# w3 times w_last by halves of the sum, with the second half's stores adding in DRAM

## The chip, the cores and the metric

The kernel runs on one core of one Trainium2 chip. The metric is the device time of one execution in microseconds (us). Beside the times there is one profiled execution, and every duration below comes from it.

## The reference

Three stages follow one another. Attention over 4 batches and 12 heads (448 positions, 64 features a head) with RMS-normalised queries and keys; a two-layer network with a leaky ReLU (768 to 2048 to 768); and a second one, whose end matters here:

```
a = x @ w1
b = x @ w2
h = a * b @ w3
return (h @ w_out).astype(np.float32)
```

All is float32, for 1792 tokens. `w3` is 1024 x 1024, and this last `w_out`, called `w_last` in the kernel, is 1024 x 768. Nothing stands between the two, so the kernel forms the product w3 times w_last once, from the weights alone, and later multiplies `a * b` by it. The change is in how that product is formed.

## The kernel before

Weights come as float64 words. Each tile of them is converted on the chip: ScalarE scales both halves of the word in place (L456, L460), VectorE shifts one and adds the other (L458, L462), and the float32 result `raw` is split into a rounded high part and the rest, a low part. For w3 these are `wh` (ScalarE, L491) and `wl` (VectorE, L198). For w_last they are `lasth` (GpSimd, L109) and `lastl` (VectorE, L198), which stay in SBUF until the product is done. Every product is then three matmuls: high by high, high by low, low by high (`group`, L532 to L549).

The product w3 times w_last has 8 row blocks of 128 rows (k). Its sum runs over 8 tiles of w_last (j). A row block's share of w3 comes as two pieces, `w3t[k, 0]` for the tiles j = 0 to 3 and `w3t[k, 1]` for j = 4 to 7, each 128 x 512. The 768 columns are cut in two (e), 384 each, one PSUM bank (`pw`) each. So one piece of w3 gives 24 matmuls of 384 columns, and the whole product 384 of them.

`combine_weights` (L552 to L579) goes row block by row block: both banks of a block stay open over both halves of the sum. Before the first piece it takes w_last's tiles 0 to 3, before the second piece tiles 4 to 7. A finished bank is copied to SBUF by ScalarE (`wo`, L575; two buffers) and stored to the DRAM tensor `wc` by a DMA that GpSimd issues (L576). `wc` is read again only in the later stages (L703, L972).

This work runs beside attention. Attention goes by pairs of heads: transposed keys (`pk`, L219), scores (`ps`, L127), the minimum and scaling on VectorE (L264), the exponential on ScalarE (L273), transposes of the result (`pt`, L307) and the product with the values (`po`, L127). ScalarE rounds the keys (`kh`, L228) and VectorE forms their rest (`kl`, L229). `fill` (L1020) deals the matmuls of the product out over attention's steps 1 to 11 by a count of their cost, and a scheduler with its own model of time then sets the final order on each engine. Each engine works through its queue in that order. The order of the weight loads and conversions is that of the list given to `Weights` (L1050 to L1063): a tile is converted when its turn in the list comes, and its load is issued some tiles ahead.

Of the kernel before, what the change touches and what calls it, by code (L numbers as in the profile page):

```python
# [11 lines left out]
AF = mybir.ActivationFunctionType  # L12
ALU = mybir.AluOpType
# [6 lines left out]
DM, FF, F2 = 768, 2048, 1024  # L20
# [6 lines left out]
K2 = F2 // P  # L27
WT = DM
PB = 2
KH2 = K2 // 2  # L30
# [18 lines left out]
def attention_then_moe(  # L49
# [22 lines left out]
    nc = tc.nc  # L72
# [19 lines left out]
    def bank(name):  # L92
        return psum.tile([P, 512], F32, tag="ps", name=name)
# [438 lines left out]
    def group(ws, ps, n, w, xs, first=True, last=True, on=False):  # L532

        wh, wl = w

        def matmul(a, x, begin, end):
            nc.tensor.matmul(ps[:, :n], a, x, start=begin, stop=end, skip_group_check=on)  # L540

        for k, (xh, xl) in enumerate(xs):
            end = last and k == len(xs) - 1
            h, l = (w[k] if isinstance(w, list) else w[:, k] for w in (wh, wl))
            matmul(h, xh, first and k == 0, False)
            matmul(h, xl, False, False)
            matmul(l, xh, False, end)
            ws.pump()
            yield 3 * n * NS  # L549


    def combine_weights(ws, pool, hi, lo):  # L552
        def last(half):
            for _ in range(KH2):
                while ws.ready <= ws.taken:
                    with tc.high_priority(CONVERT_PRIORITY if ws.ready else 0):
                        next(ws.pieces)
                    yield CONVERT_NS
                ws.take()

        n = DM // 2
        for k in range(K2):
            ps = [bank("pw") for _ in range(2)]
            for half in range(2):
                if k == 0:
                    yield from last(half)
                w = ws.take()
                js = range(half * KH2, (half + 1) * KH2)
                for e in range(2):
                    cols = slice(e * n, (e + 1) * n)  # L570
                    xs = [(hi[:, j, cols], lo[:, j, cols]) for j in js]
                    yield from group(ws, ps[e], n, w, xs, first=half == 0, last=half == 1)
            for e in range(2):
                o = pool.tile([P, n], F32, tag="o", name="wo", bufs=2)
                nc.scalar.activation(o, ps[e][:, :n], AF.Copy)  # L575
                nc.gpsimd.dma_start(  # L576
                    wc[3 * e : 3 * e + 3, :, k].rearrange("m p c -> p m c"),
                    o.rearrange("p (m c) -> p m c", m=3),
                )  # L579


# [96 lines left out]
    def sources(plan):  # L678

        for f, bs, g in plan:  # L680
            if f is first_mlp:
                tiles = [w_in[g * KG + m] for m in range(KG)] + [w_out[g, m] for m in range(NO)]
            else:
                tiles = [w12[g * KH2 + m // 2, m % 2] for m in range(2 * KH2)]
            if (f, g) in kept:
                yield from ((k, False, None, None) for k in again[f, g])
            else:
                twice = sum(x[0] is f and x[2] == g for x in plan) > 1
                names = ("", "_h", "_l") if twice else ("",)
                ks = [  # L690
                    [
                        dram.tile([P, w.shape[1] // 2], F32, name=f"kept_{f.__name__}{g}_{i}{e}")
                        for e in names
                    ]
                    for i, w in enumerate(tiles)
                ]
                kept[f, g] = [k[0] for k in ks]
                again[f, g] = [tuple(k[1:]) for k in ks]
                yield from ((w, True, k, None) for w, k in zip(tiles, ks))
            if f is second_mlp:  # L700
                for m in range(NO):
                    w = wc[m, :, g * KH2 : (g + 1) * KH2].rearrange("p k c -> p (k c)")
                    yield w, False, None, None  # L703
# [10 lines left out]
    last = {}  # L714
# [247 lines left out]
    def last_sources():  # L962
        def pairs(x):
            return list(zip(x[::2], x[1::2]))

        for g in range(NG):
            yield from pairs(kept[first_mlp, g][:KG])
            yield from ([x] for x in kept[first_mlp, g][KG:])
        for g in range(2):
            yield from pairs(kept[second_mlp, g])  # L970
            js = slice(g * KH2, (g + 1) * KH2)
            yield from ([wc[m, :, js].rearrange("p k c -> p (k c)")] for m in range(NO))  # L972
# [47 lines left out]
    def fill(gen, total, span, until, begin=0):  # L1020

        spent, n = 0.0, 0
        done = False
        while True:
            at = next(steps, None)
            n += 1
            while not done and spent < total * (n - begin) / span:
                c = next(gen, None)
                if c is None:
                    done = True  # L1030
                else:
                    spent += c
            if at is None or at == until:
                break
        for _ in gen:
            pass

    parts_of = [(first_mlp, g) for g in range(NG)] + [(second_mlp, g) for g in range(2)]
    early = [(f, (0,), g) for f, g in parts_of[:EARLY]]
    late = [(f, (1,), g) for f, g in parts_of[:EARLY]]  # L1040
# [6 lines left out]
    with tc.tile_pool(name="comb", bufs=1) as pool:  # L1047
        hi = pool.tile([P, K2, DM], F32R, name="lasth")
        lo = pool.tile([P, K2, DM], F32R, name="lastl")
        ws = Weights(  # L1050
            [
                w
                for k in range(K2)
                for h in range(2)
                for w in [
                    (w_last[j], True, None, (hi[:, j], lo[:, j]))
                    for j in range(h * KH2, (h + 1) * KH2)
                    if k == 0
                ]
                + [(w3t[k, h], True, None, None)]  # L1060
            ]
            + list(sources(early + late))
        )  # L1063
        blocks = Blocks(list(last_sources()))
        n = slots[1] - slots[0]
        fill(combine_weights(ws, pool, hi, lo), comb_ns, n * per_slot, slots[1], slots[0] * per_slot)
# [4 lines left out]
    n = PB * H + 2  # L1071
# [50 lines left out]
```

## Time and profile before

| what | value |
|---|---|
| median of 3 runs | 1182.44 us (1179.35 to 1185.0) |
| the profiled execution, its own time | 1181.46 us |
| its span, first to last instruction | 1179.7 us |
| TensorE (PE) busy | 1140.0 us, 97% |
| VectorE (DVE) busy | 705.0 us, 60% |
| ScalarE (ACT) busy | 657.8 us, 56% |
| GpSimd (POOL) busy | 228.8 us, 19% |

TensorE is busy nearly all the time, so the time is close to the sum of its work. What it loses is found in the few stretches where it stands or runs at the lower of its clocks. PEld is its loading of weights, which runs beside the matmuls. A matmul's shown duration contains its way through the array, so the spacing between starts, not the duration, says how fast a row of matmuls goes.

### The profile page before, as it was taken

The page shows a single profiled execution, that of the slowest core. Times are in us where ns is not written, and L with a number is a line of the kernel's source. Part 1 is how long each engine was busy: PE and PEld are TensorE (multiplying, and loading weights), DVE is VectorE, ACT ScalarE, POOL GpSimd, SP SyncE. Part 2 cuts the span into 40 slices and gives each one's busy share as a digit, 9 for nine tenths or more (in the row PEclk, how much of TensorE's full clock was granted, in tenths as well). Part 3 has the DMA queues.
Part 4 walks back from the last instruction along what each step waited for, and adds up shares of the span by engine and source line. Part 5 has one row for each costly group of instructions (what it writes and reads, how often), then busy time and mean ns, then how long its engine had stood idle before and what let it go on. Part 6 is the DMA issues. An engine that isn't in the chain of part 4 may idle for free.

```text
span 1179.7 us, 16734 instructions
## 1 busy us (share of the span) xinstructions
PE 1140.0 (97%) x6096; PEld 959.2 (81%) x6096; DVE 705.0 (60%) x1336; ACT 657.8 (56%) x1347; POOL 228.8 (19%) x337
## 2 busy tenths in 40 slices
PE   3899999999999999999999999999999999899998
PEld 2588866666788888888888888879999999799997
DVE  7976576877523667567545543493455556854553
ACT  7968687987644565666556543355443344443331
POOL 3331344554212232345222011000000000000000
PEclk9899999999999999999999999999999999899999
DMA  9655375885965446346342421441221212102112
GB/s 298 215 167 197 120 269 198 289 303 180 312 193 172 154 140 214 120 141 206 119 124 86 170 83 46 133 161 34 75 65 43 81 42 67 53 31 90 50 36 103
DMA packets 74979, 164.51 MB, mean 139 GB/s; under 512 B 13968, under 2 KB 42384, under 8 KB 74896
## 3 DMA queue, kind: packets, MB, share of 16 engines
q1 hardware_dynamic: 55392, 80.06, 22.2%
q10 hardware_dynamic: 10800, 48.76, 12.2%
q0 software_dynamic: 8704, 34.61, 7.8%
q8 instruction: 48, 0.79, 0.3%
q14 instruction: 35, 0.29, 0.1%
HBM read 120.46 MB, written 42.95 MB: 139 GB/s over the span
## 4 chain that ended last, share of the span: by engine, by line
PE 86%; DVE 7%; DMA 5%; issue 1%; ACT 1%; SPq 0%; POOL 0%; DVEq 0%
PE ps_mm L540 33%; PE ps_o L540 13%; PE ps_b L540 10%; PE ps L127 6%; PE pt L307 6%; PE po L127 6%; PE pw L540 5%; PE ps_c L540 5%; PE ps_a L540 2%; DVE ol L198 1%; DMA wh<-kept_first_mlp_h 1%; DMA w<-w_last 1%; DVE raw L462 1%; DMA w<-w_in 1%; PE pk L219 1%
## 5 line engine op out<-in xcount | busy, mean ns | idle before, releaser
L198 DVE TENSOR_TENSOR wl<-raw,wh 128x512 fp32r<-128x512 f32 (+1 forms) x136 | 108.3, 798 | 124.3 <-ACT wh L491 81.0
L264 DVE TENSOR_SCALAR_CACHE_REDUCE p<-ps,rs 112x448 f32<-112x448 f32 x192 | 122.3, 679 | 42.1 <-PE ps L127 41.9
L540 PE MATMUL ps_mm<-xl,wh 128*128 128x448 f32 x384 | 146.2, 381 | 0.0
L273 ACT ACTIVATE p<-p,low 112x448 f32<-112x448 f32 x192 | 126.9, 665 | 30.0 <-DVE p L264 30.0
L540 PE MATMUL ps_mm<-xh,wh 128*128 128x448 f32 x384 | 141.2, 368 | 1.9 <-DMA wh<-kept_first_mlp_h 1.9
L540 PE MATMUL ps_mm<-xh,wl 128*128 128x448 f32 x384 | 141.6, 369 | 0.7 <-DMA wl<-kept_first_mlp_l 0.7
L540 PE MATMUL ps_mm<-gl,wh 128*128 128x448 f32 x288 | 109.6, 381 | 0.0
L540 PE MATMUL ps_mm<-gh,wh 128*128 128x448 f32 x288 | 106.1, 370 | 0.5 <-DMA wh<-kept_first_mlp_h 0.5
L540 PE MATMUL ps_mm<-gh,wl 128*128 128x448 f32 x288 | 105.7, 367 | 1.0 <-DMA wl<-kept_first_mlp_l 1.0
L540 PE MATMUL ps_o<-gl,wh 128*128 128x448 f32 x288 | 104.1, 366 | 0.0
L307 PEld LDWEIGHTS pt<-ident,p 112*112 112x112 f32 x768 | 82.3, 137 | 26.5 <-issue 8.5
L456 ACT ACTIVATE w<-w 128x768 f32<-128x768 f32 (+1 forms) x80 | 63.8, 798 | 70.5 <-DMA w<-w_out 31.7
L307 PE MATMUL pt<-ident,p 112*112 112x112 f32 x768 | 96.6, 267 | 5.2 <-DVE kl L229 2.8
L540 PE MATMUL ps_o<-gh,wl 128*128 128x448 f32 x288 | 100.6, 366 | 0.0
L540 PE MATMUL ps_o<-gh,wh 128*128 128x448 f32 x288 | 99.2, 365 | 0.0
L491 ACT ACTIVATE wh<-raw 128x512 fp32r<-128x512 f32 (+1 forms) x84 | 59.4, 708 | 55.8 <-PE ps_mm L540 51.4
L540 PEld LDWEIGHTS ps_mm<-xl,wh 128*128 128x128 f32 x384 | 72.4, 188 | 12.3 <-issue 7.2
L540 PEld LDWEIGHTS ps_mm<-xh,wh 128*128 128x128 f32 x384 | 72.3, 188 | 9.0 <-DVE qk_sb L173 2.2
L746 ACT ACTIVATE wh<-raw 128x512 fp32r<-128x512 f32 (+1 forms) x52 | 36.3, 698 | 76.9 <-PE ps_b L540 33.5
L540 PEld LDWEIGHTS ps_mm<-xh,wl 128*128 128x128 f32 x384 | 72.5, 189 | 7.6 <-issue 1.6
L127 PE MATMUL po<-pth,v_sb 112*64 112x448 f32 x384 | 77.5, 546 | 1.0 <-ACT pth L105 1.0
L462 DVE CUSTOM_DVE_ANT_0 raw<-w,raw 128x1536 uint16<-128x1536 uint16 (+1 forms) x80 | 74.4, 933 | 2.0 <-ACT w L460 0.5
(139 smaller groups left out, 2524.3 us busy)
## 6 DMA issues: line engine op xcount, KB each, us to landing
w<-w_in ACTq DMA_DIRECT2D x16, 768.0 KB, 5.3
w<-w_out ACTq DMA_DIRECT2D x24, 512.0 KB, 3.9
w<-w ACTq DMA_DIRECT2D x16, 768.0 KB, 4.6
qk_sb<-qk SPq DMA_DIRECT2D x48, 224.0 KB, 4.3
w<-w3t ACTq DMA_DIRECT2D x15, 512.0 KB, 5.1
kept_first_mlp<-raw POOLq DMA_DIRECT2D x16, 384.0 KB, 5.6
kept_first_mlp<-raw POOLq DMA_DIRECT2D x24, 256.0 KB, 3.1
kept_second_mlp<-raw POOLq DMA_DIRECT2D x16, 384.0 KB, 2.9
```

The costliest lines, as they stand in the source:

```text
L127: one = nc.tensor.matmul(out, a, x, start=begin, stop=end)
L198: e.tensor_tensor(out, x, y.bitcast(F32), op=ALU.subtract)
L219: nc.tensor.transpose(pk[:, c * CP : (c + 1) * CP], kn[:, c].rearrange("p h d -> p (h d)"), ident[:CP, :CP],)
L264: nc.vector.tensor_scalar(p, ps[c % 2][e], x["scale"][:, e, c : c + 1], None, op0=ALU.mult, op1=ALU.min, accum_out=low,)
L273: exps[t] = nc.scalar.activation(p, p, AF.Exp, bias=low, scale=-1.0, accum_out=x["sums"][:, e, c : c + 1])
L307: nc.tensor.transpose(pt[:, c * CP : (c + 1) * CP], h["p"][c][:, kc * CP : (kc + 1) * CP], ident[:CP, :CP],)
L456: nc.scalar.activation(h, h, AF.Prelu, scale=2.0**-112, alpha=2.0**32)
L462: nc.vector.tensor_tensor(top, top, low, op=ALU.add)
L491: self.rounded = nc.scalar.activation(flat[0], x, AF.Copy)
L540: nc.tensor.matmul(ps[:, :n], a, x, start=begin, stop=end, skip_group_check=on)
L746: nc.scalar.activation(parts[0], x, AF.Copy)
```

## The change

The product goes in two passes. The first pass takes all 8 row blocks with w_last's tiles 0 to 3, the second all 8 with tiles 4 to 7. Only tiles 0 to 3 stand before the first piece of w3; tiles 4 to 7 are dealt out one by one before later pieces of the first pass (`late.pop(0)` at k = 2, 4, 6 and 7). A bank now holds one half of the sum for 12 matmuls and is copied out after them. So there are 32 copies and 32 stores, where there were 16 of each. The first pass stores plainly, the second with `accum_op=add`, which adds to what is in DRAM. The matmuls are the same 384.

```
     def combine_weights(ws, pool, hi, lo):
-            ps = [bank("pw") for _ in range(2)]
-            for half in range(2):
-                if k == 0:
-                    yield from last(half)
-                w = ws.take()
...
+    def combine_order():
+        early = list(range(KH2))
+        late = list(range(KH2, K2))
+        yield early, 0, 0
+        for k in range(1, K2):
+            yield ([late.pop(0)] if k % 2 == 0 or k == K2 - 1 else []), k, 0
+        for k in range(K2):
+            yield [], k, 1
...
+            w = ws.take()
+            js = range(half * KH2, (half + 1) * KH2)
             for e in range(2):
+                ps = bank("pw")
+                cols = slice(e * n, (e + 1) * n)
+                xs = [(hi[:, j, cols], lo[:, j, cols]) for j in js]
+                yield from group(ws, ps, n, w, xs)
                 o = pool.tile([P, n], F32, tag="o", name="wo", bufs=2)
-                nc.scalar.activation(o, ps[e][:, :n], AF.Copy)
+                nc.scalar.activation(o, ps[:, :n], AF.Copy)
+                sums = dict(accum_op=ALU.add) if half else {}
                 nc.gpsimd.dma_start(
                     wc[3 * e : 3 * e + 3, :, k].rearrange("m p c -> p m c"),
                     o.rearrange("p (m c) -> p m c", m=3),
+                    **sums,
                 )
...
-                for k in range(K2)
-                for h in range(2)
...
+                for js, k, half in combine_order()
+                for w in [(w_last[j], True, None, (hi[:, j], lo[:, j])) for j in js]
+                + [(w3t[k, half], True, None, None)]
```

On VectorE, right behind the low part of the first piece of w3. In these names `raw` from `w64` is a tile of w_last, `raw` from `w3` a piece of w3. Before:

```order
L198 TENSOR_TENSOR wl_479<-raw_469,wh_478 128x512
L458 TENSOR_SCALAR raw_527<-w64_400 128x768
L198 TENSOR_TENSOR lastl_156<-raw_490,lasth_155 128x768
L107 COPY pth_534<-pt_535 112x448
L173 TENSOR_TENSOR qk_sb_292<-qk_sb_292,rs_375 112x2x4x64
L462 ISA raw_527<-w64_400,raw_527 128x1536
L458 TENSOR_SCALAR raw_563<-w64_463 128x768
```

The same place now:

```order
L198 TENSOR_TENSOR wl_477<-raw_469,wh_476 128x512
L458 TENSOR_SCALAR raw_544<-w64_384 128x768
L458 TENSOR_SCALAR raw_581<-w3_386 128x512
L107 COPY pth_534<-pt_535 112x448
L462 ISA raw_544<-w64_384,raw_544 128x1536
L462 ISA raw_581<-w3_386,raw_581 128x1024
L198 TENSOR_TENSOR wl_526<-raw_489,wh_525 128x512
```

Before, tiles of w_last follow, and the second piece's `wl` stands 28 rows further on. Now it stands 6 rows further on.

On TensorE, at the product with the values of the first pair of heads (`po`) and what follows it. Before:

```order
L127 MATMUL po<-pth,v_sb 64x448 x8
L307 MATMUL pt<-ident,p 112x112 x16
L127 MATMUL ps<-kh,qh 112x448
L540 MATMUL pw<-lasth,wh 128x384
L540 MATMUL pw<-lastl,wh 128x384
```

Now:

```order
L127 MATMUL po<-pth,v_sb 64x448 x8
L307 MATMUL pt<-ident,p 112x112 x3
L540 MATMUL pw<-lasth,wh 128x384
L540 MATMUL pw<-lastl,wh 128x384
L540 MATMUL pw<-lasth,wl 128x384
```

Before, 24 matmuls of the product stand ahead of this `po`, and 24 ahead of the scores (`ps`) of the third pair. Now 60 stand ahead of the one, 84 ahead of the other, and some stand between the transposes.

On ScalarE, the copies `wo` and what they wait for (DMASW is the landing of an earlier store). Before, the second block's two copies:

```order
L575 ACTIVATE wo_928<-pw_775 128x384 [waits DMASW0_49,PE_49,Activation_49]
L152 ACTIVATE sq_974<-qk_sb_820 112x512 [waits DMAHW1_49,Activation_49]
L491 ACTIVATE wh_958<-raw_944 128x512 [waits PE_49]
L437 DMA w3_1021<-w3t 128x1024 [waits DMAHW7_49]
L575 ACTIVATE wo_931<-pw_776 128x384 [waits DMASW1_49,PE_49]
```

Now, where the third pair's exponentials run:

```order
L579 ACTIVATE wo_760<-pw_723 128x384 [waits DMASW3_49]
L273 ACTIVATE p_802,sum_785<-p_802,low_803 112x448 [waits DVE_49]
L273 ACTIVATE p_806,sum_785<-p_806,low_807 112x448 [waits DVE_49]
L579 ACTIVATE wo_823<-pw_763 128x384 [waits DMASW4_49,Activation_49]
L273 ACTIVATE p_810,sum_785<-p_810,low_811 112x448 [waits DVE_49]
L491 ACTIVATE wh_1005<-raw_987 128x512 [waits PE_49]
L437 DMA w3_1050<-w3t 128x1024 [waits DMAHW5_49]
L273 ACTIVATE p_814,sum_785<-p_814,low_815 112x448 [waits DVE_49]
L579 ACTIVATE wo_846<-pw_826 128x384 [waits DMASW5_49,PE_49,Activation_49]
```

There are twice as many copies, and each waits for the landing of the store two before it, with attention's exponentials queued behind.

## Rows read from the trace of the kernel before

**Rows 1.** Page: busy us, share of span, instructions of each engine.

```profile
PE 1140.0 (97%) x6096; PEld 959.2 (81%) x6096; DVE 705.0 (60%) x1336; ACT 657.8 (56%) x1347; POOL 228.8 (19%) x337
```

**Rows 2.** Stretches: us, length, busy us of each engine, PE clock, DMA share, GB/s.

```profile
38.30:49.10 10.80, 10.76 (x64) 6.75 (x60) 10.80 (x19) 10.80 (x26) 4.55 (x4) 1.00 0.38 133
49.10:51.80 2.70, 0.00 (x0) 0.00 (x0) 2.70 (x5) 1.73 (x4) 1.20 (x1) 1.00 0.89 188
51.80:58.60 6.80, 6.57 (x23) 4.53 (x24) 6.80 (x16) 5.03 (x10) 1.91 (x2) 0.50 0.47 148
...
62.00:160.40 98.40, 98.40 (x596) 80.18 (x594) 60.66 (x130) 70.42 (x158) 27.89 (x44) 1.00 0.56 180
```

**Rows 3.** Waits of PE, 0 to 62 us: in total, times, longest.

```profile
PE pt L307 <- DVE kl L229: 2.8, 1, 2.8
...
PE ps L127 <- ACT wh L491: 0.2, 1, 0.2
```

**Rows 4.** Chain that ended last, 52 to 54 us: start, us, what.

```profile
52.40 0.64 ACT wh L491
53.04 0.70 PE ps L127
```

**Rows 5.** Timeline of PE: start, us, engine, line, operation, count.

```profile
41.80 0.44 PE L540 MATMUL pw<-lasth,wh 128*128 128x384 f32 x1
42.17 0.45 PE L127 MATMUL ps<-kh,qh 64*112 64x448 f32 x1
...
54.15 0.52 PE L540 MATMUL pw<-lastl,wh 128*128 128x384 f32 x1
54.47 0.52 PE L540 MATMUL pw<-lasth,wh 128*128 128x384 f32 x1
...
155.14 0.33 PE L540 MATMUL pw<-lasth,wl 128*128 128x384 f32 x1
155.31 0.34 PE L540 MATMUL pw<-lasth,wh 128*128 128x384 f32 x1
155.58 0.45 PE L127 MATMUL ps<-kh,qh 64*112 64x448 f32 x1
```

**Rows 6.** Timeline of DVE: first and second piece's low part, a wide tile's add.

```profile
36.80 0.69 DVE L198 TENSOR_TENSOR wl<-raw,wh 128x512 fp32r<-128x512 f32 x1
...
39.91 0.95 DVE L462 CUSTOM_DVE_ANT_0 raw<-w,raw 128x1536 uint16<-128x1536 uint16 x1
...
55.55 0.68 DVE L198 TENSOR_TENSOR wl<-raw,wh 128x512 fp32r<-128x512 f32 x1
```

**Rows 7.** Timeline of ACT, 47 to 56 us.

```profile
47.18 0.68 ACT L228 ACTIVATE kh<-pk,gqk 128x448 fp32r<-128x448 f32 x1
...
48.34 0.73 ACT L273 ACTIVATE p<-p,low 112x448 f32<-112x448 f32 x1
...
48.99 0.65 ACT L152 ACTIVATE sq<-qk_sb 112x512 f32<-112x512 f32 x1
49.52 0.69 ACT L152 ACTIVATE qk_sb<-qk_sb 112x512 f32<-112x512 f32 x1
...
54.96 0.68 ACT L456 ACTIVATE w<-w 128x512 f32<-128x512 f32 x1
55.53 0.67 ACT L460 ACTIVATE w<-w 128x512 uint32<-128x512 uint32 x1
```

**Rows 8.** Copies and stores of the product: ns min/median/max, first and last start.

```profile
L575 ACT ACTIVATE wo<-pw x16: 461/470/493, 60.9 to 163.1; 128x384 f32<-128x384 f32 x16
L576 POOL DMA_DIRECT2D wc<-wo x16: 748/796/993, 61.7 to 164.4; - x16
...
DMA to landing us min/median/max: 2.5/4.4/8.1
```

**Rows 9.** DMA issues, 0 to 165 us: KB each, median us to landing.

```profile
w<-w_last ACTq DMA_DIRECT2D x4, 768.0 KB, 8.7
```

More of the change, by code (lines that the diff above doesn't have):

```diff
@@ L549, in group @@
             yield 3 * n * NS
+    def combine_order():
[6 more added lines that the diff above has]
+            yield [], k, 1
     def combine_weights(ws, pool, hi, lo):
-        def last(half):
-            for _ in range(KH2):
+        n = DM // 2
+        for new, k, half in combine_order():
+            for _ in new:
                 while ws.ready <= ws.taken:
@@ L559, in last @@
                 ws.take()
-        n = DM // 2
-        for k in range(K2):
-            ps = [bank("pw") for _ in range(2)]
-            for half in range(2):
-                if k == 0:
-                    yield from last(half)
-                w = ws.take()
[L568 to L572, printed above, removed]
+            w = ws.take()
+            js = range(half * KH2, (half + 1) * KH2)
             for e in range(2):
+                ps = bank("pw")
+                cols = slice(e * n, (e + 1) * n)
+                xs = [(hi[:, j, cols], lo[:, j, cols]) for j in js]
+                yield from group(ws, ps, n, w, xs)
                 o = pool.tile([P, n], F32, tag="o", name="wo", bufs=2)
-                nc.scalar.activation(o, ps[e][:, :n], AF.Copy)
+                nc.scalar.activation(o, ps[:, :n], AF.Copy)
+                sums = dict(accum_op=ALU.add) if half else {}
                 nc.gpsimd.dma_start(
@@ L1052, in attention_then_moe @@
                 w
-                for k in range(K2)
-                for h in range(2)
[L1055 to L1060, printed above, removed]
+                for js, k, half in combine_order()
+                for w in [(w_last[j], True, None, (hi[:, j], lo[:, j])) for j in js]
+                + [(w3t[k, half], True, None, None)]
             ]
```

## Prediction

> **What bounds the kernel now.** The page comes first. TensorE (PE) is busy 97% of the span [rows 1], so a change gains only where PE stands or runs slowly, and the next view is the one by stretches [rows 2]. From 62 to 160.4 us, where most of this product is done, PE is busy in all of 98.40 us at a granted clock of 1.00: nothing to gain there. Before it there are two places. Between 49.1 and 51.8 us PE does nothing, and from 51.8 to 58.6 its granted clock is 0.50, the lower of its two levels (1.2 GHz). The matmuls show it: two of 384 columns start 0.32 us apart at 54.15, and 0.17 us apart at 155.14 [rows 5]. The waits name what PE stood for: a transpose 2.8 us for `kl`, the third pair's keys on VectorE, and the scores behind it 0.2 us more, with `wh`, the second piece of w3, ending last [rows 3]. The chain of what ended last runs into PE at 53.04 from `wh` [rows 4]. VectorE is busy throughout (10.80 of 10.80, 2.70 of 2.70): four tiles of w_last pass through it there. From the first piece's low part at 36.80 to the second's at 55.55 are 18.75 us [rows 6], and with the first piece's 24 matmuls done PE has nothing of the product to fill a gap with.
>
> **The change part by part.** All sums are made against the profiled execution, 1181.46 us, of which its span is 1179.7; that is 0.98 us under the median of 1182.44.
>
> What goes: the standing, 2.8 + 0.2 = 3.0 us [rows 3], and the slow stretch after it, in which 6.57 us of work [rows 2] would take half: 3.3 us. Together 6.3 us, if PE has work through the whole of it.
>
> Has it? By the order now, 84 matmuls of the product stand ahead of the third pair's scores instead of 24. These 60 take 60 x 0.17 = 10.2 us at the upper clock [rows 5], more than the 6.3 that are to be filled. Their weights: the second piece's low part stands 6 rows behind the first's on VectorE. At no more than 0.95 us each, the widest add there [rows 6], it ends by 36.80 + 0.69 + 6 x 0.95 = 43.2 us, where PE still has the first piece and attention. So late `wh` is no longer what PE meets.
>
> What is late next is ScalarE. Before, it finishes the third pair's `kh` from 47.18 us [rows 7]. By the order now, it does more ahead of that: 3 narrow tiles at 2 x 0.57, 4 roundings (0.57 each, as one pass over such a tile), 3 copies at 0.47 [rows 8], 2 exponentials at 0.65 and 2 squares at 0.53, the spacings of rows 7: 3.4 + 2.3 + 1.4 + 1.3 + 1.1 = 9.5 us, so `kh` starts near 56.7 and `kl` is ready near 58. PE reaches these scores at 53.0 [rows 4] less the 3.0 of standing plus 10.2: 60.2 us. Two us are in hand. That is little, because ScalarE must wait for loads there; I charge 1.0 us for short waits of PE, between 0 (all within the two us) and 6.3 (the gap comes back whole).
>
> What is added. Sixteen copies of 0.47 us on ScalarE, 7.5 us: it stands 28 of the 98.4 us in which most of them fall [rows 2], so nothing; without that cover 7.5. Sixteen stores that GpSimd takes 0.80 us each to issue [rows 8], 12.8 us beside some 70 in which it stands [rows 2]: nothing. Behind them on GpSimd are queued the small factors of the next pairs and the low parts `ql` and `xl`, which are needed a pair later. More changes of PE between the product and attention: 98 instead of 90 up to its last matmul. One costs 0.27 - 0.17 = 0.10 us [rows 5], so 0.8 us. SP's queue issues the same loads; of ScalarE's, pieces of w3 go out earlier and tiles of w_last later, out of a full stretch into one at a DMA share of 0.38 [rows 2]: nothing.
>
> The open cost is the added wait. There are two buffers `wo`, and each copy waits for the landing of the store two before it, with attention's exponentials queued behind on ScalarE. Two copies can't follow faster than copy, issue and landing: 0.47 + 0.80 + 4.4 = 5.7 us [rows 8]. What PE leaves for it follows from the copies before: sixteen, each of a bank of 24 matmuls, start from 60.9 to 163.1 us [rows 8], so 24 matmuls, now two banks, come every 102.2 / 15 = 6.8 us, with attention between. The plain stores of the first pass fit. The second pass's stores add in DRAM, and no row shows such a store. It can't gain. The nearest row is the plain store of the same 192 KB on the same queue, 4.4 us; at the upper end I set twice that, 8.8, because it also reads what it writes. At 4.4 it costs nothing; at 8.8 two copies take 10.1 us, 3.3 more than PE leaves, over eight such pairs 26.4 us. I take 5.5, near the plain store's row: 6.8 us, just fitting.
>
> Sum: -6.3 + 0.8 + 1.0 = -4.5 us, or 1177.0 us for a profiled execution and 1178.0 us against the median.
>
> **The rivals.** *PE had more slack than its busy time shows.* In the 10.80 us from 38.3 PE counts as busy for 10.76, but its weight loads fill 6.75 us, 63%; from 62 to 160.4 they fill 80.18 of 98.40, 81% [rows 2]. At 81% the same loads fit in 8.3 us, so 2.5 us of that stretch are short waits between matmuls. Rows 5 have one: from `pw` at 41.80 to `ps` at 42.17 are 0.37 us, where the same step takes 0.27 at 155.31. With work of the product at hand they would go too: -4.5 - 2.5 = -7.0, 1175.4 us. Against it: the kinds of matmul differ between the stretches (short transposes load more often), and attention's own chain through ScalarE and VectorE stays.
>
> The Trainium skill has this as a rule ("Perfetto Trace Analysis", section "Identifying the Most-Contended Engine"): matmul busy time is a poor measure of how near TensorE is to its peak, and the busy share of its weight loads a better one. The two stretches of rows 2 agree with it as far as 10.76 of 10.80 busy goes with 63% of loading; by busy time alone the sum stays at -4.5, by the rule it is -7.0.
>
> *ScalarE takes the place of VectorE.* From 38 us to the third pair's scores it has no free time by the count above, and it must wait there for tiles of w_last whose loads are now issued later, one at a time; such a load takes 8.7 us to land [rows 9]. Two such waits of 3 us use up the 2 us in hand and the gain: about 0, 1182 us, give or take 2. For it speaks how full the engine is; against it, that the DMA engines are less busy by then (0.38).
>
> *The adding stores bind.* Place: the copies of the second pass on ScalarE, with attention's exponentials behind them. The price is 8 x (L + 1.27 - 6.8) for a landing of L us. It begins at L = 5.5, has used up the gain of 4.5 at 6.1, and is slower by over 0.5% from 6.8. At 8.8 it is -4.5 + 26.4 = +22: 1204 us. For it: the slowest plain store took 8.1 us [rows 8], and an adding one does more. Against it: the banks PE can fill meanwhile, and that two stores are under way at once.
>
> **How the numbers follow.** The forecast has 0.40, the first rival 0.27, the second 0.15, the third 0.18. A measurement of this kernel can tell about 0.5%, 5.9 us, from no change. Faster by more than that is most of the first rival (0.25) and the better edge of the forecast (0.05): 0.30. Slower is most of the third rival (0.14) and a little of the second (0.01): 0.15. The rest, 0.55, is within. The likeliest case alone spans 1175.5 to 1180 us. The range goes from 1173 (below it 0.05, the edge of the first rival) to 1192 (above it 0.10, where adding stores land after 7.3 us or more).
>
> **What would show it.** Right: no standing of PE at 49 us; its granted clock at 1.00 from 40 us on; 84 matmuls of the product ahead of the third pair's scores, which start near 60 us; the last matmul of the product near 156 us (before, the stretch of rows 2 that ends at 160.4 ends with it); 32 copies, the later stores landing within 6 us; the orders behind it shifted as a whole. Wrong: a wait of PE for ScalarE's `kh` or exponentials, or for a bank, between 45 and 75 us (second rival); ScalarE's copies waiting for DMA after 90 us and PE idle behind them (third); weight loads above 75% before 62 us and a gain of 7 (first).

## The result, and the profile after

The changed kernel takes 1190.35 us (median of 11 runs, 1187.18 to 1194.3), the kernel before 1182.44 us over as many runs on that chip (1178.07 to 1187.82). The ratio is 1.0064, with a 95% interval of 1.0048 to 1.0080: 7.6 us slower, where 4.5 us less were forecast. The time lies within the range that was given, but on the other side of the kernel before. The profiled execution took 1190.86 us, its span 1189.1 us.

First the page's busy times and its row of GpSimd's own DMA queue (packets, MB, share of the 16 engines' span), which answer to [rows 1]:

```profile
PE 1141.7 (96%) x6096; PEld 958.9 (81%) x6096; DVE 700.7 (59%) x1336; ACT 663.4 (56%) x1363; POOL 251.8 (21%) x353
...
q0 software_dynamic: 15104, 37.76, 10.3%
```

TensorE (PE) has the same work. GpSimd's queue moves 3.1 MB more, as 16 more stores should, but in 15104 packets instead of 8704. Next the stretches, those of [rows 2] and two more (columns as there):

```profile
20.00:40.00 20.00, 9.57 (x40) 6.47 (x39) 15.68 (x33) 15.61 (x31) 5.18 (x5) 0.50 0.90 275
...
38.30:49.10 10.80, 10.80 (x58) 9.53 (x57) 8.70 (x16) 10.80 (x25) 4.20 (x7) 0.81 0.83 242
49.10:51.80 2.70, 2.70 (x17) 2.70 (x17) 2.70 (x7) 2.70 (x6) 1.83 (x3) 1.00 0.90 352
51.80:58.60 6.80, 6.80 (x41) 4.42 (x40) 4.88 (x10) 6.80 (x16) 2.77 (x3) 1.00 0.57 190
...
112.00:168.00 56.00, 51.98 (x302) 41.20 (x301) 34.95 (x71) 37.89 (x88) 31.07 (x38) 0.95 0.90 191
```

and the two added stretches in the kernel before:

```profile
20.00:40.00 20.00, 13.54 (x64) 10.30 (x63) 20.00 (x38) 20.00 (x43) 7.91 (x10) 1.00 1.04 349
112.00:168.00 56.00, 56.00 (x342) 44.00 (x341) 36.13 (x78) 38.64 (x88) 21.48 (x33) 1.00 0.57 191
```

Three things can be read. What the forecast wanted is there: PE no longer stands from 49.1 to 51.8 us, and from 51.8 to 58.6 its granted clock is 1.00 (2.4 GHz). But ahead of that, from 20 to 40 us, ScalarE (ACT) is busy for 15.61 us instead of 20.00 and VectorE for 15.68: 4 us are lost before the product begins. And from 112 to 168 us PE loses 4.0 us that it did not lose before, at a DMA share of 0.90 instead of 0.57, and its granted clock is 0.95 in the mean instead of 1.00. Of the times that the prediction named, the third pair's scores start at 63.59 us (forecast near 60).

**The start.** ScalarE's timeline (start, us; ACTq rows are DMA issues; in brackets the idle time and what ended it), then two links of the chain that ended last:

```profile
14.94 0.38 ACTq L437 DMA_DIRECT2D w<-w3t  x1
15.54 0.33 ACTq L437 DMA_DIRECT2D w<-w_last  x1
17.37 0.34 ACTq L437 DMA_DIRECT2D w<-w3t  x1
20.02 4.12 ACTq L437 DMA_DIRECT2D w<-w3t  x2
24.19 0.67 ACT L273 ACTIVATE p<-p,low 112x448 f32<-112x448 f32 x1 [3.41 <-DMA v_sb<-v]
...
36.57 0.63 ACT L491 ACTIVATE wh<-raw 128x512 fp32r<-128x512 f32 x1
```

```profile
9.20 14.59 DMA v_sb<-v
23.81 0.33 ACTq L437
24.19 0.18 ACT p L273
```

The second of the two issues at 20.02 does not go out until `v`, issued by SP at 9.20 us, has landed at 23.79. While this load instruction waits, all of ScalarE stands: the exponential behind it starts 3.41 us late. (`v` itself landed hardly earlier before, at 23.52 us; what came earlier in ScalarE's queue is the load that waits for it.) The same stretch before holds only this ahead of 23 us, and `wh` comes 4.06 us sooner:

```profile
15.49 0.38 ACTq L437 DMA_DIRECT2D w<-w_last  x1
21.09 0.38 ACTq L437 DMA_DIRECT2D w<-w3t  x1
21.59 0.40 ACTq L437 DMA_DIRECT2D w<-w3t  x1
...
32.51 0.65 ACT L491 ACTIVATE wh<-raw 128x512 fp32r<-128x512 f32 x1
```

So by 20.5 us ScalarE has sent for 2.25 MB (three pieces of w3 and a tile of w_last) instead of 0.75, into engines that are already full (a DMA share of 1.05 from 14 to 21 us, before 1.03), and the second pair's `qk` share these engines with them (its last one lands at 30.94 us, before at 26.78). The Trainium skill ("DMA: Bandwidth & Descriptors", section "Issuing engines are not separate DMA queues") says that starting transfers from several engines saves only the time of the issue; the trace agrees in that SP's `qk`, issued at 13.00 us and so ahead of ScalarE's pieces, took 17.94 us to land, where it took 13.25 before.

**The second pass.** The stores of `wc` from 40 to 108 us, nearly all plain, then those from 107 to 180 us, which add (the store at 107.2 us, the first that adds, is in both and has the 1316 ns and the 7.2 us of the first; ns min/median/max of the issue, first and last start; then who waited, us and times):

```profile
L581 POOL DMA_DIRECT2D wc<-wo x17: 762/797/1316, 49.3 to 107.2; - x17
...
ACT wo L579: 6.5, 5
...
DMA to landing us min/median/max: 2.5/3.7/7.2
```

```profile
L581 POOL DMA_DIRECT2D wc<-wo x16: 1259/1356/1806, 107.2 to 171.1; - x16
...
ACT wo L579: 8.9, 5
...
DMA to landing us min/median/max: 3.9/5.2/8.2
```

An adding store of the same 192 KB takes GpSimd 1.36 us to issue instead of the 0.80 of [rows 8], and 5.2 us to land in the median. ScalarE's copies wait for landings nine times in both passes together, 15.3 us. PE's waits up to 200 us show what reached it, as [rows 3] did before:

```profile
PE ps L127 <- ACT wo L579: 5.3, 3, 2.6
PE pt L307 <- ACT p L273: 3.6, 1, 3.6
PE pw L540 <- issue: 3.5, 1, 3.5
```

The first row is the copies: scores that need the bank a late copy holds. It was not there before; 1.3 us of it lie in the first pass, at 74.79 us, and 4.0 in the second. The other two are the start (2.4 and 1.8 us before). Behind the waits PE also runs slowly: the granted clock is 0.92 in the mean from 70 to 112 us (see `a_plain` below), and at the end of the product

```profile
160.00:168.00 8.00, 7.37 (x27) 5.18 (x27) 5.11 (x12) 6.64 (x16) 5.50 (x6) 0.62 0.83 182
```

where the kernel before has 1.00 and 52 matmuls. The last matmul of the product starts at 167.11 us; before, at 160.17.

### The profile page after: what moved, and what is told of

Same layout as the page of the kernel before. It is cut to its first block, busy times and chain, and to the rows that moved or that the text cites. A ratio compares the mean times of both kernels' runs of the same rounds, so it can differ in the third digit from the quotient of the medians.

```text
span 1189.1 us, 16789 instructions
## 1 busy us (share of the span) xinstructions
PE 1141.7 (96%) x6096; PEld 958.9 (81%) x6096; DVE 700.7 (59%) x1336; ACT 663.4 (56%) x1363; POOL 251.8 (21%) x353
## 3 DMA queue, kind: packets, MB, share of 16 engines
q0 software_dynamic: 15104, 37.76, 10.3%
## 4 chain that ended last, share of the span: by engine, by line
PE 74%; DMA 9%; ACT 5%; DVE 5%; issue 4%; POOL 2%; SPq 0%; ACTq 0%; POOLq 0%; DVEq 0%
PE ps_mm L540 29%; PE ps_o L540 13%; PE ps_b L540 9%; PE ps_c L540 5%; PE ps L127 5%; PE po L127 5%; PE pt L307 4%; PE ps_a L540 2%; DMA w<-w_out 2%; PE pw L540 2%; DMA wc<-wo 1%; ACT p L273 1%; DMA v_sb<-v 1%; DMA wh<-kept_first_mlp_h 1%; DVE ol L198 1%
## 5 line engine op out<-in xcount | busy, mean ns | idle before, releaser
L752 ACT ACTIVATE wh<-raw 128x512 fp32r<-128x512 f32 (+1 forms) x52 | 36.3, 698 | 74.3 <-PE ps_b L540 33.7
L540 PE MATMUL ps_b<-oh,wh 128*128 128x448 f32 x192 | 71.5, 372 | 2.6 <-ACT wh L752 2.1
```

What stands on the lines that cost most here:

```text
L752: nc.scalar.activation(parts[0], x, AF.Copy)
```

## The experiments

Each is timed beside the kernel before on the same chip; ratios are to that kernel, with 95% intervals. The theory that grew out of the traces: the gain came as forecast, and two costs outweigh it, the pieces of w3 loaded early and the adding stores. `a_plain`, `f_both_undone` and `j_like_before_plain` leave out the sum of the two halves; the others compute it.

| kernel | ratio | interval | first product of w3, us |
|---|---|---|---|
| changed | 1.0064 | 1.0048 to 1.0080 | 37.3 |
| `g_changed` | 1.0077 | 1.0051 to 1.0102 | 38.0 |
| `a_plain` | 1.0004 | 0.9983 to 1.0024 | 36.8 |
| `b_bufs4` | 1.0018 | 0.9998 to 1.0039 | 37.4 |
| `c_loads` | 1.0031 | 1.0013 to 1.0049 | not read |
| `e_loads_bufs4` | 0.9983 | 0.9964 to 1.0002 | 32.5 |
| `f_both_undone` | 1.0024 | 1.0002 to 1.0045 | 36.9 |
| `h_rows5` | 1.0007 | 0.9989 to 1.0026 | 36.4 |
| `h_rows4` | 1.0014 | 0.9998 to 1.0030 | 36.7 |
| `i_like_before` | 1.0020 | 0.9997 to 1.0043 | 33.4 |
| `j_like_before_plain` | 0.9940 | 0.9919 to 0.9961 | 33.5 |
| `k_like_before_bufs4` | 0.9977 | 0.9954 to 1.0001 | 33.1 |
| `m_add_later` | 0.9987 | 0.9972 to 1.0002 | 33.2 |
| `m_add_later_b4` | 0.9969 | 0.9954 to 0.9983 | 33.3 |
| `n_add_past_400` | 0.9931 | 0.9910 to 0.9953 | 33.7 |

**The adding alone, and the tiles alone.**

```
a_plain:   - sums = dict(accum_op=ALU.add) if half else {}
           + sums = {}
b_bufs4:   - name="wo", bufs=2
           + name="wo", bufs=4
```

> The changed kernel with plain stores in the second pass: the sum of the two halves is left out, all else and the order on every engine are the same. Theory A, the adding is what costs from 112 to 168 us (GpSimd took 1.36 us to issue an adding store against 0.80, landing 5.0 us against 3.7): issue about 0.80, landing about 3.7 in the second pass too, TensorE's waits for the copies (5.3 us) mostly gone, 4 to 7 us faster than the changed kernel, near 1184 us. Theory B, twice as many stores through two buffers cost it, adding or not: within 1.5 us of the changed kernel. Either way the first matmul of the product stays near 37.3 us.

> The changed kernel with four copy buffers instead of two. If the loss of the second pass comes through copies that wait for landings (A and B both): ScalarE's 15.3 us of waits for stores gone, TensorE's 5.3 us behind them too, 4 to 6 us faster than the changed kernel, near 1185 us. If it comes from GpSimd being held 1.36 us by each adding store, which delays its other work: no more than 1.5 us. First matmul of the product near 37.3 us in both.

Plain stores, in the same order on every engine, are 7.1 us faster than the changed kernel (1.0064 to 1.0004). The stretch in which they fall, in `a_plain`:

```profile
112.00:168.00 56.00, 55.24 (x356) 43.56 (x354) 41.62 (x89) 43.85 (x104) 27.31 (x47) 1.00 0.70 226
```

PE has 55.24 of 56 us again, at a DMA share of 0.70. So by the times the adding costs 7 us, and without it the change is still worth nothing. Not all that sets the two traces apart is the adding, though. Up to the first adding store at 107.2 us the two kernels are the same, and yet the changed kernel loses time there that `a_plain` does not; nor does `b_bufs4`. In this order (changed, `a_plain`, `b_bufs4`):

```profile
70.00:112.00 42.00, 40.70 (x230) 33.17 (x228) 22.84 (x52) 32.47 (x74) 14.06 (x22) 0.92 0.62 195
...
70.00:112.00 42.00, 42.00 (x253) 32.94 (x252) 26.43 (x60) 33.97 (x78) 13.18 (x19) 1.00 0.65 208
...
70.00:112.00 42.00, 42.00 (x261) 33.63 (x260) 27.20 (x63) 36.71 (x83) 16.53 (x21) 1.00 0.72 211
```

In the changed kernel PE stood at 74.79 us for a copy that had waited for a plain store, and ran slowly behind it. The second pair's product with the values starts at 85.43 us there (84.10 in `g_changed`), at 80.42 in `a_plain` and at 80.19 in `b_bufs4`. The profiled execution of `a_plain` took 1180.15 us where the median is 1183.88, so how often plain stores cost these 4 to 5 us is not shown.

Four tiles with adding stores give back 5.4 us (1.0064 to 1.0018), and there no copy waits for a landing. But the second pass of `b_bufs4` loses as much of PE as with two tiles:

```profile
112.00:168.00 56.00, 52.18 (x332) 41.34 (x331) 37.93 (x78) 38.90 (x91) 32.77 (x44) 1.00 0.94 213
...
PE ps L127 <- ACT wo L579: 2.0, 1, 2.0
PE pt L307 <- ACT pth L105: 1.8, 1, 1.8
```

The copy that PE waits for here is late behind a weight load (`w_out`) that took 8.36 us to land. So what the four tiles give back can be read in this pair of traces only ahead of the adding stores (80.19 for 85.43 us) and in the clock (1.00 for 0.95). That the wait for a tile is the larger part of the adding's price is not shown.

**The early loads, a first try, which went wrong.**

```
c_loads:  - after = max(last[home].pop(0), t - 7, -4 if t < 5 else 0)
          + after = max(last[home].pop(0), t - (5 if t < 12 else 7), ...)
e_loads_bufs4 is this and bufs=4; f_both_undone is this and sums = {}
```

> The changed kernel with the loads of tiles 5 to 11 issued no more than five tiles ahead instead of seven, so that fewer loads are out at once at the start. Theory C, the start lost 4 us because a load instruction in ScalarE's queue waited from about 20 to 24 us for an older transfer: ScalarE no longer stands there, the first matmul of the product comes at 33 to 34 us instead of 37.3, and it is 3 to 5 us faster than the changed kernel, near 1186 us. Rival: the DMA engines are full until 38 us, so what is not waited for there is waited for a little later: first matmul at 36 to 38 us, within 1.5 us.

> Both: later loads and four copy buffers. If the two losses are separate, the gains add: 8 to 10 us faster than the changed kernel, about 1181 us, level with the kernel before or up to 2 us faster. If one takes the place of the other: no more than 6 us faster, 1184 us or above.

> The changed kernel with both suspected costs away and still two output tiles: the early loads of w3 go out five tiles ahead, not seven, and the second half's stores don't add (the sum of the halves is left out). Theory (the loss is these two and nothing else, and they add up): the adding alone gave back 0.60% and the loads with four tiles 0.35% of the time, so 1190.35 x (1 - 0.0095) = about 1179 us, a ratio to the kernel before of 0.997 (0.995 to 0.999); the first product of w3 starts near 32.5 us, the copies wait under 4 us for landings, and TensorE is busy over 55 of the 56 us from 112 to 168. Rival one (they overlap: what one stall takes the other would have taken anyway): about the 1183.9 of the plain stores alone, ratio 1.000. Rival two (a third cost, such as the 16 more copies and changes of kind, eats the gain that was forecast): ratio 1.000 or more even with the first product early. The forecast's own sum, without the two failed terms, asks for 4.5 us under before, ratio 0.996.

> The changed kernel as it is, beside the others on one chip, so that the differences need no second chip: 0.64% over before (1.0048 to 1.008), 1190 us. Theory: the difference to the kernel with both costs undone is 0.9 to 1.0%. Rival: under 0.7%, if the costs overlap.

Of `c_loads` only the times are used; its order is that of `f_both_undone` on every engine. Times first looked like two costs that add up: 3.9 us for the loads (`c_loads`), and with four tiles 9.6 us in all (`e_loads_bufs4`). `f_both_undone` then should have come to 0.997 and came to 1.0024. The reason stands in two stretches of the two traces, of `f_both_undone`:

```profile
20.00:40.00 20.00, 10.26 (x42) 7.25 (x41) 17.23 (x36) 16.25 (x36) 5.44 (x5) 0.50 0.90 266
160.00:168.00 8.00, 5.42 (x24) 3.47 (x25) 6.02 (x12) 4.09 (x11) 3.18 (x8) 0.65 0.47 136
```

and of `e_loads_bufs4`:

```profile
20.00:40.00 20.00, 14.21 (x59) 10.87 (x58) 19.59 (x38) 20.00 (x44) 9.49 (x10) 0.56 0.85 276
160.00:168.00 8.00, 6.65 (x34) 5.18 (x36) 6.17 (x18) 6.56 (x18) 0.14 (x1) 0.55 0.23 59
```

ScalarE's first 75 instructions are the same in both, yet in one the start is lost (16.25 of 20 us busy) and in the other it is not (20.00): with a tile of w_last and three pieces of w3 still sent out by 21 us, it depends on the execution whether the second pair's loads come in time. So one trace of such a start proves little, and the edit had not removed the cause. It also moved later work: both lose PE time and clock from 160 to 168 us, `f_both_undone` though its stores are plain and no copy held PE up. This experiment therefore tested neither theory nor rival. `g_changed` confirms the size of the loss on that chip.

**Fewer rows by halves.**

```
h_rows5:  rows k < 5 by halves (10 adding stores), rows 5 to 7 in one sum
h_rows4:  the same with k < 4 (8 adding stores); both with bufs=4 and the loads of c_loads
```

> Only the first five rows of w3 go by halves (10 adding stores instead of 16, six fewer copies and stores), the other three as before in one sum; four output tiles, early loads five tiles ahead, so it is complete and computes the reference. Theory: what is left of the cost of adding with four tiles is the adding stores' share of the DMA engines and of GpSimd, about 1.7 us for 16, so 10 leave 1.1 us; the tiles of w_last then come due every 4 to 8 us, which VectorE still makes: 1181.5 us, ratio 0.998 (0.995 to 1.000). Rival: the rows not yet halved are needed to cover w_last's later tiles, and TensorE stands again between 70 and 100 us for 2 to 4 us: ratio 1.001.

> The same with the first four rows by halves (8 adding stores). Theory: as with five rows, with 0.2 us less for adding but w_last's second half due one after another in 4 us each: ratio 0.998 to 1.001. Rival: as much adding cost as with 16, since the one landing that binds stays: the same as with 16 and four tiles, 0.998. If it stands for w_last instead, the trace shows TensorE waiting for VectorE's wl between 60 and 80 us.

Neither is faster than `e_loads_bufs4`, and 1.0007 is near the rival's number, but the rival's sign is not there: from 70 to 100 us PE is busy in all of 30.00 us in both. What `h_rows5` loses lies ahead of that, 27.84 of 30 us from 40 to 70, where `e_loads_bufs4` has 30.00:

```profile
PE pw L540 <- ACT wh L491: 2.2, 1, 2.2
```

This wait is at 45.72 us, behind a start that was late as well (36.4 us). So these two settle neither the theory nor the rival.

**The early loads, put back where they were.** Only the tiles t = 5 to 8 of the list get another place; SyncE's order stays the same, PE's differs from the changed one in few places.

```
i_like_before:
- after = max(last[home].pop(0), t - 7, -4 if t < 5 else 0)
+ after = max(last[home].pop(0), {5: 2, 6: 0, 7: 2, 8: 2}.get(t, t - 7), -4 if t < 5 else 0)
j_like_before_plain:  and sums = {}
k_like_before_bufs4:  and bufs=4
l_before_again:       the kernel before, unchanged
```

> The changed kernel, with the early loads of ScalarE's queue put back near where the kernel before has them (one tile of w_last, and the pieces of w3 only behind the loads of the second pair, instead of three pieces of w3 ahead of them); SyncE's instructions stay the same, and the other engines nearly. Theory: the pieces of w3 ahead hold up the second pair's loads and with them ScalarE, 3.6 to 4.7 us in four traces, so the first product of w3 starts near 33.5 us instead of 37, and the ratio to the kernel before falls from 1.0064 to 1.003 (1186.5 us); the copies still wait for the adding stores, 12 to 15 us in all. Rival: a full stretch gives that time to some other transfer whatever is put first, the first product starts at 36 to 37 us all the same, as it did with the loads five tiles ahead (36.9), and the ratio stays at 1.006.

> The same with the second half's stores plain (the sum of the halves is left out), two output tiles as before: both suspected costs are away without another order. Theory: what the forecast asked for without its two failed terms, 4.5 us under before, ratio 0.9965 (0.995 to 0.998), 1178 us. Rival one (the start is not to be had): 1.000, as with plain stores alone. Rival two (the gain ahead of the third pair is spent later whatever is done): 1.000 although the first product starts near 33.5 us.

> The same with adding stores and four output tiles: complete, computes the reference. Theory: no copy waits for a landing, what is left of the adding is 1.7 us of crowding on the DMA engines, so ratio 0.998 (0.996 to 1.000), 1180 us, as the kernel with four tiles and loads five ahead had by a good draw of its start. Rival: 1.002, as with four tiles alone, if the start does not come back.

> The kernel before, unchanged, for a second look at its start. Theory: the first product of w3 near 33.3 us again (within 1 us), v and qk of the second pair landed by 27 us. Rival: that start was a good draw, and it comes out at 35 us or later here; then the loss of 3.6 us at the start is not the change's.

All three theories' ratios came, `j_like_before_plain` even lower; the copies of `i_like_before` waited less than expected, 6.9 us in all instead of 12 to 15. ScalarE in `i_like_before`:

```profile
15.19 0.38 ACTq L437 DMA_DIRECT2D w<-w_last  x1
20.27 0.83 ACTq L437 DMA_DIRECT2D w<-w3t  x2
22.75 0.33 ACTq L437 DMA_DIRECT2D w<-w3t  x1
...
31.20 0.63 ACT L491 ACTIVATE wh<-raw 128x512 fp32r<-128x512 f32 x1
```

One load ahead of 20 us instead of three, no wait, and `wh` 5.4 us sooner than in the changed kernel. All six kernels with these loads start the product at 33.1 to 33.7 us; the kernel before did so at 33.3 and, in `l_before_again`, at 32.6. The four traces of the changed start (changed, `g_changed`, `a_plain`, `b_bufs4`) have 36.8 to 38.0. In time the loads are worth 5.2 us with adding stores (1.0064 to 1.0020) and 7.6 us with plain ones (1.0004 to 0.9940). With both costs gone the change gains 0.60%, 7.1 us.

**Amount or place of the adding?** `k_like_before_bufs4` has no copy waiting for a landing and is still 4.4 us behind plain stores. Its second pass:

```profile
112.00:168.00 56.00, 52.08 (x305) 40.37 (x305) 36.76 (x76) 37.13 (x87) 31.12 (x40) 0.91 0.90 211
```

Again a DMA share of 0.90 and 4 us of PE lost. (This execution took 1186.30 us where the median is 1179.46, so its losses are more than the usual ones. But PE is busy for only 51.98 to 52.64 us here in all six traces with 16 adding stores, with two tiles or four, and for 54.88 to 55.52 in the five of `a_plain`, `j_like_before_plain` and the three kernels below, whose second pass stores plainly.) The next kernels do the same adding later, from DRAM to DRAM:

```
m_add_later:   the second half's stores go plain to wc2; then, one m behind each of
               six later kept tiles in GpSimd's queue (kept > 20):
+ nc.gpsimd.dma_start(wc[m], wc2[m], accum_op=ALU.add, max_dma_last_dim=1024)
m_add_later_b4:  and bufs=4
n_add_past_400:  m_add_later_b4 with kept > 28
```

> The loads as in the last three, two output tiles; the second half's stores go plain to a second array in DRAM, and six transfers from DRAM to DRAM add that array to the first behind later stores of GpSimd's queue, after the last product of w3 and ahead of the first read of the sum near 570 us. Complete, computes the reference; 3.1 MB more are moved than with adding stores. Theory (the adding costs by its place: a copy, a bank and a full stretch stand behind it from 112 to 168 us): the same as the plain stores, ratio 0.994 (0.992 to 0.996), 1175.5 us, since the DMA engines are busy 0.4 of the stretch from 400 to 780 us and 0.7 from 168 to 400. Rival (it costs by its amount, wherever it stands, through GpSimd's issue and the DMA engines' time): some of the 4 to 9.5 us that lie between adding and plain stores comes back, ratio 0.997 or more.

> The same with four output tiles instead of two. With plain stores copies still wait 7.1 us for landings, of which TensorE waits 1.0 us: if that is the last of it, ratio 0.993, a microsecond under the one with two tiles; the rival, that the tiles cost nothing once the stores are plain, gives the same 0.994.

> The later adding again, with four output tiles, but its six transfers stand eight converted tiles later, past 400 us, where the DMA engines are busy 0.47 of the time instead of the 0.90 to 1.07 from 280 to 320 us. Complete. Theory (place, not amount): the 4 us that TensorE lost from 300 to 320 us waiting for the first layer's kept weights don't come back, so ratio 0.994 (0.992 to 0.996), 1175 us, and no wait for kept weights over 2 us before 400 us. Rival (amount): 0.997 as with the adding near 300 us, the wait only moved to other loads past 400 us.

`m_add_later` did not come to 0.994, nor `m_add_later_b4` to 0.993. The trace of `m_add_later` keeps the whole gain up to 293 us and loses half of it by 340; the stretch, then PE's waits from 280 to 420 us:

```profile
300.00:320.00 20.00, 14.19 (x70) 11.46 (x69) 4.90 (x12) 7.66 (x18) 6.16 (x10) 0.91 1.14 294
```

```profile
PE ps_mm L550 <- DMA wh<-kept_first_mlp_h: 5.0, 2, 4.6
```

The added transfers had met another full stretch, and PE stood for the first layer's weights (2.4 us before). In `n_add_past_400` the six transfers go out from 416 to 457 us:

```profile
300.00:320.00 20.00, 18.20 (x101) 15.96 (x101) 4.37 (x11) 9.05 (x21) 5.98 (x9) 1.00 0.79 249
400.00:480.00 80.00, 78.99 (x442) 65.29 (x442) 53.75 (x101) 48.16 (x101) 27.85 (x36) 1.00 0.74 193
```

From 400 to 480 us PE stands 1.0 us, none of it for a load. The ratio is 0.9931, 8.2 us under the kernel before, though 3.1 MB more are read and 3.1 MB more written than in the changed kernel. This kernel computes the whole reference and beats both: 1175.26 us (1174.02 to 1179.77).

## Why the prediction was wrong

By its own steps:

- **What goes: 6.3 us.** Right in place. PE does not stand at 49 us and runs at 1.00 through the old slow stretch. The size fits too: with both costs away 7.1 us are gained (interval 4.6 to 9.6) and in `n_add_past_400` 8.2, where 6.3 less 0.8 for the changes of PE are 5.5. The first rival's 7.0 fits as well, and these intervals do not tell them apart. Its mark, weight loads above 75%, is misleading in the changed kernel: of the 9.53 us of loading in the 10.80 us from 38.3, 3.99 fall into 4.1 us at a granted clock of 0.50, and there are 57 loads where the kernel before has 60 [rows 2]. At 1.00 throughout it can be read in `j_like_before_plain`:

```profile
38.30:49.10 10.80, 10.80 (x67) 9.62 (x66) 10.69 (x23) 10.80 (x21) 4.66 (x5) 1.00 0.88 311
```

  That is 89% after 63%, with 66 loads after 60. Most of the difference is their kind: 46 of them are the product's, of 188 ns each, where the kernel before has 20 of these and 28 short ones of transposes and products with the values, of 133 to 136 ns. By the weight-load rule of the Trainium skill ("Perfetto Trace Analysis", section "Identifying the Most-Contended Engine") the stretch had room that busy time does not show. This trace doesn't contradict it, and no run here tests it.
- **"What is late next is ScalarE", charged 1.0 us.** No such wait: in the changed kernel PE is busy in 30.00 of the 30 us from 40 to 70, and the second rival (ScalarE in VectorE's place) did not come. The charge should have been nothing.
- **"Of ScalarE's, pieces of w3 go out earlier and tiles of w_last later, out of a full stretch into one at a DMA share of 0.38: nothing."** This failed first. The sentence follows the tiles of w_last, which did leave the full stretch, and forgets that the pieces of w3 moved into it: three of them, 1.5 MB, are out by 20.5 us, at a DMA share of 1.05, before the second pair's loads have landed. The runs put 5.2 to 7.6 us in the place of nothing.
- **The open cost, "just fitting".** This failed second: the adding cost 7.1 to 9.5 us where the sum had nothing, and the third rival's signs came, copies waiting for DMA after 90 us and PE idle behind them. Of the sum's own terms the landing was nearly right (5.5 taken, 5.2 in the median), but the issue, charged at a plain store's 0.80, took 1.36. By these medians two copies take 0.49 + 1.36 + 5.2 = 7.05 us against 6.8, or 8 x 0.25 = 2.0 us over the pass, which is too little. Two things had no term. One is the slow stretch behind a wait: the step charged it for the old gap, but not for the new ones (0.62 from 160 to 168 us). The other is the crowd of adding stores on the DMA engines, which four tiles leave (4 us of PE from 112 to 168 us with them too) and a later adding takes away (1.0020 to 0.9977 to 0.9931). How the 7.1 to 9.5 us are shared among these stays open.
- **"The plain stores of the first pass fit."** Not in every execution. In the changed kernel's two traces PE stood 1.3 and 0.9 us for copies of the first pass, and with the slow stretch behind that the second pair's product with the values came 5.0 and 3.7 us later than in `a_plain`. Why it came there and not in `a_plain` is not shown: the slowest plain store of that pass landed after 5.6 us in the changed kernel and after 6.2 in `a_plain`.

Together: from the 7.1 us gained in `j_like_before_plain` to the 7.6 lost are 14.7 us. In the one sequence of undoing the adding is 7.1 and the loads 7.6; in the other the loads are 5.2 and the adding 9.5. The difference between the two, 2.4 us, is within the intervals, some 2.5 us for each ratio.

What stays open, beside the shares named above, is how often the kernel with loads five tiles ahead loses its start; the two traces shown differ by 4.4 us.

## What to carry to other kernels

When a list of weights is put in another order, follow every load that becomes earlier, not only those that become later, and look at the DMA share of the stretch that it moves into and at what stands behind it in that engine's queue. A transfer that no row prices is to be bounded in its issue, its landing and its load on the shared engines apart, and held against the closest pair of uses, not against their mean distance. What a wait of PE costs is the standing and, where one follows, the slow stretch behind it (`b_bufs4` had none behind its waits from 112 to 168 us, the changed kernel did); a sum that counts both for the wait that goes has to ask for both for the waits that may come. An adding that nobody reads soon can be done later, in a stretch where the DMA engines are half idle.

## What the runs showed of the hardware

An adding store of 192 KB takes 400 packets where a plain one takes 64: 16 plain stores more bring q0 from 8704 to 9728 packets in `a_plain`, and the same stores adding bring it to 15104. In the stretch from 112 to 168 us the DMA share was 0.90 at 191 GB/s with adding stores, and 0.70 at 226 GB/s with plain ones. From DRAM to DRAM, 512 KB were added in 8.6 us (6.1 to 11.2) in a half idle stretch, and in 10.5 us (up to 15.7) where the stretch was fuller (`m_add_later`).

The clock's column is to be read with the spacing of the matmuls. In the kernel before it shows 1.00 from 20 to 40 us in one execution and 0.59 in `l_before_again`, with 64 matmuls in each, and in both two matmuls of 384 columns start 0.32 us apart (33.72 and 34.04; 33.07 and 33.39), as at 1.2 GHz.
